# Picking the first rows by matrix multiply, and a first layer on the whole array, in the opening of a fused convolution and feed-forward kernel

## The chip, the cores and the metric

The kernel runs on one core of a Trainium2 chip. The metric is device time in microseconds (us) of one execution; the numbers are medians of several executions of the compiled program. The profile is of one execution by the hardware profiler. Its span starts and ends a little inside the timed interval (733.2 us of span for a run of 734.93).

PE is TensorE (matmuls), PEld its weight loads, ACT is ScalarE, DVE is VectorE, POOL is GpSimd, SP the sync engine, which here only issues DMAs.

## The reference, cut to what matters

```python
# x: (8, 4096, 192), weight_gen: (8, 4096, 8 heads, 7 taps), both float32
w = softmax(weight_gen, axis=-1)
x_pad = pad x by 6 zero rows in front of each sequence
out[b, s, h, :] = sum over k of w[b, s, h, k] * x_pad[b, s + k, h, :]     # 24 channels a head
h = relu(out.reshape(32768, 192) @ w_in)      # w_in  (192, 2048)
return (h * h) @ w_out                        # w_out (2048, 192)
```

Nearly all the arithmetic is in the two matrix products. The convolution has weights of its own for every position. The kernel turns it into matmuls as well, with a band of softmax weights as the moving operand.

## The kernel before: the parts that matter

The 32768 tokens are cut into sub-blocks of 512. The first two blocks are one sub-block each, so that work can start early; all later blocks are two. A block goes through these steps: softmax, rows of weights (`wr`), bands (`bd`), convolution (`yp` in PSUM, copied to `y`), 8 or 16 *units* of the first layer (`h`), each followed by a ScalarE relu (`t`) and a VectorE square (`g`), then the second layer (`o`).

The softmax has 8 consecutive positions in each partition. The bands need one position in each partition. In the kernel before, DMA does this re-arrangement (cuts are marked with `...`):

```python
def wr_load_sbuf(j, parts, order, engines):
    wr_t[j] = p_wr.tile([P, NT, HP, SL * 2], f16, name="wr")
    ...
    for i in order:                     # five overlapping tiles of 128 positions
        ...
        engines[n % len(engines)].dma_start(out=wr_t[j][a - t0 : b - t0, i]..., in_=s.v[...])
```

The opening, before the first block:

```python
spin(25)                                # warm-up matmuls on zeros
half_swap(); band_mask()
s0.load(nc.sync); load_w_in(w_st[0], 0, nc.sync); x_load_f32(0); load_w_in(w_st[1], 1, nc.sync)
s0.exp(...); s0.total(...); s0.recip(...); s0.scale(...)
nc.scalar.copy(out=w_i[:, 0, 0], in_=w_st[0])            # w_in, first half, float32 to float16
wr_load_sbuf(0, [s0], (0, 2, 1, 4, 3), (nc.sync, nc.gpsimd))
wr_load_sbuf(1, [s0], range(NT), (nc.gpsimd,))
x_cast(0, nc.scalar.copy)
cross_w_in_by_pe(0)                     # copy of w_in with its 64-row halves exchanged
spin(14)
x_load_f32(1)
nc.scalar.copy(out=w_i[:, 1, 0], in_=w_st[1])
cross_w_in(1)
...
```

A unit contracts over 192 rows in 64-row halves. Two 64-row matmuls lie side by side on the array, one working for each half of the tokens. This is why a crossed copy of w_in must exist:

```python
for jj in range(per):                   # per is 2 in the first two blocks
    for slot in range(NK):              # 3 slots of 64 rows
        for half, r0 in enumerate((0, RT)):
            k = slot ^ half if slot < 2 else slot
            nc.tensor.matmul(out=h[:, half, jj*th:(jj+1)*th], lhsT=w_in_chunk(...),
                             rhs=y_t[j][r0:r0+RT, k, 0:th], tile_position=(r0, 0), ...)
```

The softmax here doesn't subtract the row's maximum and nothing guards it: scores larger than these inputs give would overflow.

Of the kernel before, what the change touches and what calls it, by code (L numbers as in the profile page):

```python
# [9 lines left out]
def kernel(  # L10
# [26 lines left out]
    nc = tc.nc  # L37
    f32 = mybir.dt.float32
# [10 lines left out]
    PAIRED_FROM = 4  # L49
# [7 lines left out]
    NBLK = len(BLOCKS)  # L57
    NF = Dff // P
# [11 lines left out]
    bounds = [0, 104, 208, 312, 416, TB]  # L70

# [26 lines left out]
    swap = const.tile([P, P], f16, name="swap")  # L98
    FIRST = 8
    PARTS = {0: (8, 8, 8, 8), 1: (8, 8, 16), 2: (16, 16)}  # L100
# [5 lines left out]
    def half_swap():  # L106

        nc.gpsimd.memset(swap, 0.0)
        for base in (RT, -RT):
            nc.gpsimd.affine_select(  # L110
                out=swap, in_=swap, pattern=[[-1, P]], compare_op=AluOp.not_equal,
                fill=1.0, base=base, channel_multiplier=1,
            )
# [28 lines left out]

    def cross_w_in_by_pe(q):
        n = NQ + NQ // 2
        for a in range(0, n, 2 * TB):
            b = min(a + 2 * TB, n)
            pt = ps_h.tile([P, 2 * TB], f32, name="pt", tag="h")
            for c in range(a, b, TB):
                nc.tensor.matmul(
                    out=pt[:, c - a : c - a + TB], lhsT=swap, rhs=w_i[:, q, 0, c : c + TB],  # L150
                    start=True, stop=True,
                )
            nc.scalar.copy(out=w_i[:, q, 1, a:b], in_=pt[:, 0 : b - a])
# [147 lines left out]
    x_t, wr_t, bd_t, yp_t, y_t, g_t, gp_t, t1_t, o_t, o_sb_t = ({} for _ in range(10))  # L301
# [68 lines left out]

    def st_band(j, tiles):


        if j not in bd_t:
            bd_t[j] = p_bd.tile([P, H * NT * STEP], f16, name="bd")
        i = tiles[0]
        lo = STEP * i
        shift = 0 if i == 0 and j % NBB == 0 else lo - tile_start(j, i)
        n = min(STEP, P - shift)
        shape = (P, HP * len(tiles), n // SL, 2 * SL)  # L380
        nc.vector.tensor_tensor(  # L381
            out=bd_t[j][:, H * lo : H * (lo + len(tiles) * n)].rearrange(
                "p (g m c) -> p g m c", g=shape[1], c=2 * SL
            ),
            in0=wr_t[j][:, i : tiles[-1] + 1]
            .rearrange("p t g c -> p (t g) c")
            .unsqueeze(2)
            .broadcast_to(shape),
            in1=mask[:, shift : shift + n]
            .rearrange("p (m c) e -> p m (c e)", c=SL)  # L390
            .unsqueeze(1)
            .broadcast_to(shape),
            op=AluOp.mult,
        )
# [7 lines left out]
    def conv_pieces(j):  # L402


        s0, n = BLOCKS[j]
        th = n * TB // 2
        halves = []
        for half in (0, 1):
            s, a = (s0 + half, 0) if n == 2 else (s0, th * half)
            halves.append([  # L410
                (s, i, half, max(bounds[i], a), min(bounds[i + 1], a + th), a)
                for i in range(NT) if bounds[i] < a + th and bounds[i + 1] > a
            ])
        if n == 2:
            for k in range(NK):
                for later in (True, False):
                    for pair in zip(*halves):
                        for s, i, half, a, b, base in pair:
                            for q in (2 * k, 2 * k + 1):
                                yield later, s, i, q, half, a, b, base  # L420
        else:
            for pair in zip(*halves):
                for later in (True, False):
                    for k in range(NK):
                        for s, i, half, a, b, base in pair:
                            for q in (2 * k, 2 * k + 1):
                                yield later, s, i, q, half, a, b, base
# [38 lines left out]
    def st_conv(j):  # L466

        if j >= FIRST_SPREAD:
            return st_conv_spread(j)
        n = BLOCKS[j][1]  # L470
        th = n * TB // 2
        per = 1024 // th
        y = p_y.tile([P, NK, TB], f16, name="y")
        y_t[j] = y
        yps = [
            ps_h.tile([P, 2 * TB], f32, name="yp", tag="h") for _ in range(-(-NK // per))
        ]
        for later, s, i, q, half, a, b, base in conv_pieces(j):
            lo = bounds[i]
            hi = lo + (STEP if tile_start(s, i) == starts[i] else bounds[i + 1] - lo)  # L480
            _, ha, hb, pre = quads[q]
            m, h = (32, hb) if later else (pre, ha)
            bd = bd_t[s][:, H * lo : H * hi].rearrange("p (g c e) -> p g e c", g=HP, e=2)
            p0 = RT * half + 32 * (q % 2)
            k = q // 2
            col = th * (k % per) - base
            nc.tensor.matmul(  # L487
                out=yps[k // per][p0 : p0 + m, col + a : col + b],
                lhsT=x_t[s][:, i, 32 * q : 32 * q + m],
                rhs=bd[:, h // 2, h % 2, a - lo : b - lo],  # L490
                start=True,
                stop=True,
                skip_group_check=True,
                tile_position=(0, p0),
            )
        for n, yp in enumerate(yps):
            k0, k1 = n * per, min((n + 1) * per, NK)

            copies = ((k0, k1, nc.scalar.copy),)
            if j == 0:  # L500
                copies = ((0, 2, nc.scalar.copy), (2, NK, nc.vector.tensor_copy))
            for a, b, copy in copies:
                copy(  # L503
                    out=y[:, a:b, 0:th],
                    in_=yp[:, (a - k0) * th : (b - k0) * th].rearrange("p (k c) -> p k c", c=th),
                )

    def st_unit(j, u):

        th = BLOCKS[j][1] * TB // 2  # L510
        per = TB // th
        w = w_p if j >= FIRST_SPREAD else w_i
        h = ps_h.tile([P, 2, TB], f32, name="h", tag="h")
        for jj in range(per):
            for slot in range(NK):
                for half, r0 in enumerate((0, RT)):
                    k = slot ^ half if slot < 2 else slot
                    nc.tensor.matmul(  # L518
                        out=h[:, half, jj * th : (jj + 1) * th],
                        lhsT=w_in_chunk(w, u * per + jj, slot, half),  # L520
                        rhs=y_t[j][r0 : r0 + RT, k, 0:th],
                        start=(jj == 0 and slot == 0), stop=(slot == NK - 1),
# [10 lines left out]
        n = 2 if PAIRED_FROM <= j and u < NF - 2 else 1  # L533
# [14 lines left out]
    def st_mm2(j, qt, fcs, ccs, o):  # L548


        th = BLOCKS[j][1] * TB // 2
        per = TB // th
        half, off = divmod(qt * QT, th)
        for fc in fcs:
            g = g_t[(j, fc // per)][:, half, fc % per * th + off :]
# [39 lines left out]
    with nc.allow_low_precision("fp16 matmul pipeline"), tc.manual_schedule():  # L595
# [20 lines left out]
        nc.vector.memset(warm, 0.0)  # L616
        for v in v_first:
            nc.vector.memset(v, 0.0)
# [3 lines left out]
        def spin(n):  # L622
# [4 lines left out]
        spin(25)  # L627
        half_swap()
        band_mask()
        nc.gpsimd.memset(v_big, 0.0)  # L630
        s0.load(nc.sync)
        w_st = [
            p_wg.tile([P, (R + HALO) * HK], f32, name="w_st", tag="wg")[:, 0 : NQ + NQ // 2]
            for q in (0, 1)
        ]
        load_w_in(w_st[0], 0, nc.sync)
        x_load_f32(0)
        load_w_in(w_st[1], 1, nc.sync)
# [4 lines left out]
        nc.scalar.copy(out=w_i[:, 0, 0], in_=w_st[0])  # L643
        wr_load_sbuf(0, [s0], (0, 2, 1, 4, 3), (nc.sync, nc.gpsimd))
        wr_load_sbuf(1, [s0], range(NT), (nc.gpsimd,))
        x_cast(0, nc.scalar.copy)
        cross_w_in_by_pe(0)
        spin(14)
        x_load_f32(1)
        nc.scalar.copy(out=w_i[:, 1, 0], in_=w_st[1])  # L650
        cross_w_in(1)
        s1.load(nc.sync)
        for i in (0, 2, 1, 3, 4):
            st_band(0, (i,))
        st_conv(0)

        nc.gpsimd.tensor_copy(out=gate, in_=x_st[1][:, 0:1])
        for q in range(4):
            load_w_out(q, 4)
        s2.load(nc.gpsimd)  # L660
        x_load(2)

# [6 lines left out]
            0: "B1 X1 u u u E1 S1 u C u u u u",  # L669
            1: "L3 u u B2 M E2 B3 u M E2 u u S2 u M u C u S2 M",  # L670
            2: "L4 u u u E3 M u u u M B4 u u u u M B5 S3 u u u u M u E3 C u",
            3: "L5 L6 M S3 u u u M u u u u M u M B6 E4 u u u M M B7 u u u E4 M u M C S4 u",
# [95 lines left out]
        def quarters():  # L768

            for j in range(NBLK - 1):  # L770
                for qt in range(2 * BLOCKS[j][1]):
                    o = new_o(ps_o, 1, qt % 2) if j < 2 else new_o(ps_o)
                    st_mm2(j, qt, FCS[0], (0, 1), o)
                    yield
                    st_mm2(j, qt, FCS[1], (0, 1), o)
                    o_sum(j, qt, (0, 1), o)
                    if qt % 2:
                        o_store(j, qt - 1, range(4), nc.sync)
                    yield

        mm2 = quarters()
        for j in range(NBLK):
            if j + 2 < NBLK:
                load_rows(j + 2)
            u = 0
            for step in plans[j].split():
# [25 lines left out]
                elif kind == "X":  # L812
                    x_cast(n, nc.vector.tensor_copy)
# [47 lines left out]
```

## Time and profile before

| | kernel before |
|---|---|
| time, median | 734.86 us (734.37 to 736.79) |
| TensorE busy | 99% of the span |
| first unit of the first layer starts | 16.03 us |
| convolution of block 2 starts | 33.87 us |
| convolution of block 4 starts | 76.05 us |

The three last rows are marks. They are the starts of matmul groups in the timeline. Block 4 is the first that the two kernels reach with the same work behind them. What is left after that mark is the same in both.

The prediction shows the lines that say where the time lies. In the chain in order of time (start, us, what), three units in a row:

```profile
29.68 2.07 PE h L518 x36
```

That is 2.07 / 3 = 0.69 us a unit.

### The profile page before, as it was taken

Reading aid. Unit: us, or ns where it says so; the run is one execution under the profiler, and the core shown is the slowest. Engines: PE = TensorE matmul, PEld = TensorE weight load, DVE = VectorE, ACT = ScalarE, POOL = GpSimd, SP = SyncE. Lnnn points to the kernel's source line nnn. Section 1 sums busy time; section 2 is a strip of 40 time slices with the busy share of each in tenths; the row PEclk is TensorE's granted clock in tenths of the full one; section 3 lists DMA queues with packets and bytes.
Section 4 is the critical chain, followed back from the end, with each engine's and each line's share of the span. In section 5 each row is a group of like instructions: output and inputs, shape, how many; then the busy total and the mean of one; then the engine's idle time right before and its main releaser. Section 6 shows DMA issues by size and latency. Waiting matters only on the chain.

```text
span 733.2 us, 31124 instructions
## 1 busy us (share of the span) xinstructions
PE 726.3 (99%) x14106; PEld 528.5 (72%) x14106; DVE 627.3 (86%) x856; ACT 613.8 (84%) x724; POOL 100.5 (14%) x148
## 2 busy tenths in 40 slices
PE   8999999999999999999999999999999999999998
PEld 4767777777777777777777777777777777777777
DVE  5999898998898988888988888988889988778753
ACT  5998888988888888888888888888888888888883
POOL 7322222320001100011000010010100110001000
PEclk9999999999999999999999999999999999999999
DMA  7745444794445442455433464334544315444012
GB/s 216 124 88 132 81 63 106 143 164 119 93 73 117 105 86 64 71 131 112 69 70 72 115 125 82 62 68 122 104 87 85 59 49 120 66 87 78 30 45 67
DMA packets 126544, 68.71 MB, mean 94 GB/s; under 512 B 85193, under 2 KB 122636, under 8 KB 125900
## 3 DMA queue, kind: packets, MB, share of 16 engines
q1 hardware_dynamic: 80908, 48.12, 23.0%
q0 software_dynamic: 45360, 18.50, 21.6%
q8 instruction: 110, 1.80, 1.0%
q14 instruction: 22, 0.18, 0.1%
q10 hardware_dynamic: 144, 0.10, 0.0%
HBM read 50.18 MB, written 28.70 MB: 108 GB/s over the span
## 4 chain that ended last, share of the span: by engine, by line
PE 96%; DVE 1%; DMA 1%; ACT 1%; issue 0%; DVEq 0%
PE o L560 47%; PE h L518 45%; PE yp L450 4%; PE yp L487 1%; DVE bd L381 1%; DMA wr<-v_first 1%; ACT t L532 0%; DMA wg<-in_weight_gen_dram 0%; ACT ex L250 0%; DVE v_first L272 0%; ACT y L503 0%; DVE ssum L257 0%; DVE rcp L264 0%; DVE g L536 0%; DVE xt L347 0%
## 5 line engine op out<-in xcount | busy, mean ns | idle before, releaser
L532 ACT ACTIVATE t<-h 128x1024 f16<-128x1024 f32 x512 | 496.5, 1026 | 59.9 <-PE h L518 59.5
L560 PEld LDWEIGHTS <-g 64*128 64x128 f16 (+1 forms) x8032 | 342.5, 94 | 55.9 <-issue 2.5
L560 PE MATMUL o<-w_o,g 64*128 64x192 f16 (+1 forms) x8032 | 379.0, 243 | 0.0
L536 DVE TENSOR_TENSOR g<-t 128x2048 f16<-128x2048 f16 (+1 forms) x309 | 309.3, 1037 | 28.1 <-ACT t L532 27.9
L518 PE MATMUL h<-y,w_p 64*128 64x512 f16 x2400 | 291.7, 376 | 0.0
L518 PEld LDWEIGHTS <-w_p 64*128 64x128 f16 x2400 | 113.8, 94 | 94.9
L381 DVE TENSOR_TENSOR bd<-wr,mask 128x4160 f16<-128x4160 f16 (+3 forms) x89 | 149.4, 1703 | 4.1 <-DMA wr<-v_first 4.1
L576 DVE TENSOR_TENSOR o_sb<-o,o_sb 128x384 f32<-128x384 f32 x123 | 68.4, 556 | 60.8 <-ACT o_sb L574 59.8
L333 POOL DMA_DIRECT2D xt<-in_x_dram x62 | 52.1, 843 | 421.6 <-PE yp L450 362.5
L574 ACT COPY o_sb<-o 128x384 f32<-128x384 f32 x129 | 61.6, 478 | 46.7 <-PE o L560 45.9
L518 PE MATMUL h<-y,w_i 64*128 64x512 f16 (+1 forms) x768 | 82.1, 350 | 1.8 <-ACT t L532 0.8
L518 PEld LDWEIGHTS <-w_i 64*128 64x128 f16 x768 | 36.1, 94 | 28.6 <-issue 4.0
L450 PEld LDWEIGHTS <-xt 128*32 128x32 f16 x2000 | 24.5, 95 | 10.6 <-issue 10.6
L272 DVE TENSOR_TENSOR v_big<-ex,rcp 128x112 f16<-128x112 f32 (+5 forms) x180 | 29.8, 236 | 1.8 <-DMA vd<-v_big 0.8
L460 DVE CAST y<-yp 128x1024 f16<-128x1024 f32 x25 | 30.4, 1218 | 0.0
L450 PE MATMUL yp<-bd,xt 128*32 128x104 f16 (+1 forms) x2000 | 28.3, 210 | 0.0
L250 ACT ACTIVATE ex<-wg 128x560 f32<-128x560 f32 (+4 forms) x38 | 25.9, 682 | 1.7 <-DMA wg<-in_weight_gen_dram 1.7
L257 DVE TENSOR_REDUCE ssum<-ex 128x80 f32<-128x560 f32 (+4 forms) x38 | 25.3, 666 | 2.2 <-ACT ex L250 2.2
L460 ACT CAST y<-yp 128x1024 f16<-128x1024 f32 x25 | 25.2, 1006 | 0.0
L264 DVE RECIPROCAL rcp<-ssum 128x80 f32<-128x80 f32 (+4 forms) x38 | 22.8, 600 | 1.3
L323 POOL DMA_DIRECT2D xt<-in_x_dram x7 | 3.9, 553 | 124.7 <-PE yp L450 109.7
L363 POOL DMA_DIRECT2D wr<-v_first x31 | 16.9, 563 | 16.0 <-DVE v_first L272 15.8
(34 smaller groups left out, 97.3 us busy)
## 6 DMA issues: line engine op xcount, KB each, us to landing
out_dram<-o_sb SPq DMA_DIRECT2D x63, 384.0 KB
xt<-in_x_dram POOLq DMA_DIRECT2D x42, 240.0 KB, 5.0
wg<-in_weight_gen_dram SPq DMA_DIRECT2D x4, 1064.0 KB
xt<-in_x_dram POOLq DMA_DIRECT2D x20, 192.0 KB, 4.7
wr<-vd SPq DMA_DIRECT2D x38, 80.0 KB
vd<-v_big SPq DMA_DIRECT2D x5, 512.0 KB
y<-y SPq DMA_DIRECT2D x100, 24.0 KB
wg<-in_weight_gen_dram SPq DMA_DIRECT2D x5, 392.0 KB
```

The lines of the kernel that those rows point to most:

```text
L250: nc.scalar.activation(out=self.ex[:, lo:hi].rearrange("p r g k e -> p (r g) k e"), in_=self.wg[:, lo:hi].rearrange("p r (g e) k -> p (r g ...
L272: eng.tensor_tensor(out=bass.AP(tensor=v.tensor, offset=v.offset + lo * H * SL + lo % SL * 2 + g * SL * 2, ap=[list(v.ap[0]), [H * SL + 2, ...
L333: eng.dma_start(out=dst[:, first:last], in_=ap)
L381: nc.vector.tensor_tensor(out=bd_t[j][:, H * lo : H * (lo + len(tiles) * n)].rearrange("p (g m c) -> p g m c", g=shape[1], c=2 * SL), in0= ...
L450: nc.tensor.matmul(out=yp[p0 : p0 + 32, k - k0, a:b], lhsT=x_t[s][:, i, c0 : c0 + 32], rhs=bd[:, head // 2, e, 0 : b - a], start=True, sto ...
L460: copy(out=y[:, k0 : k0 + 2], in_=yp)
L518: nc.tensor.matmul(out=h[:, half, jj * th : (jj + 1) * th], lhsT=w_in_chunk(w, u * per + jj, slot, half), rhs=y_t[j][r0 : r0 + RT, k, 0:th ...
L532: nc.scalar.activation(out=t1[:, e], in_=h, func=ActF.Relu)
L536: nc.vector.tensor_tensor(out=g[:, a : e + 1], in0=t1[:, a : e + 1], in1=t1[:, a : e + 1], op=AluOp.mult)
L560: nc.tensor.matmul(out=oo[:, cc * Dm : (cc + 1) * Dm], lhsT=g[r0 : r0 + n, cc * P : (cc + 1) * P], rhs=w_o[r0 : r0 + n, fc, :], start=(fc ...
L574: nc.scalar.copy(out=o_sb, in_=o[0][:, c])
L576: nc.vector.tensor_tensor(out=o_sb, in0=o[1][:, c], in1=o_sb, op=AluOp.add)
```

## The change

Its intent is to bring the first useful matmul forward. The rows of the first two sub-blocks are picked by TensorE with a 0/1 selection matrix instead of by DMA. The first two blocks' units use the whole array for 128 of the 192 rows, so that no crossed copy of w_in is needed before block 2. The second half of w_in, x of the second sub-block and the second part of the softmax weights (a part serves two sub-blocks, so this one is for block 2) are loaded by GpSimd, the first two casting on the way. Squares are done two units at a time in all blocks. Some second-layer work moves from block 3 to block 0. The diff, cut to its core:

```diff
+    def select_rows(j, s, tiles, places):
+        ...
+        for i, (pool, tag) in zip(tiles, places):
+            pr = pool.tile([P, H * SL], f32, name="pr", tag=tag)
+            for r in range(s.r):                                  # 8
+                nc.tensor.matmul(out=pr, lhsT=sel[:, c : c + P], rhs=s.v[:, HALO + r]...,
+                                 start=(r == 0), stop=(r == s.r - 1))
+    def copy_rows(j, tiles):
+        for i in tiles:
+            nc.scalar.copy(out=wr_t[j][:, i]..., in_=pr_t.pop((j, i)))
...
+    def first_unit(u, h, y):
+        both  = [...]   # two 128-row matmuls of 512 columns
+        upper = [...]   # two 64-row matmuls of 512 columns, side by side
+        pairs = (upper, both) if u % 2 else (both, upper)
...
-        n = 2 if PAIRED_FROM <= j and u < NF - 2 else 1
+        n = 2 if j < NFIRST or u < NF - 2 else 1
...
-        spin(25)
-        half_swap()
+        spin(21)
+        row_select()
-        load_w_in(w_st[1], 1, nc.sync)
+        load_w_in(w_i[:, 1, 0], 1, nc.gpsimd)
+        x_load(1)
+        s1.load(nc.gpsimd)
-        wr_load_sbuf(0, [s0], (0, 2, 1, 4, 3), (nc.sync, nc.gpsimd))
-        wr_load_sbuf(1, [s0], range(NT), (nc.gpsimd,))
-        cross_w_in_by_pe(0)
-        spin(14)
+        select_rows(0, s0, ROW_ORDER, (o1, ring, ring, ring, o0))
+        copy_rows(0, ROW_ORDER)
+        def next_rows(i):                       # runs behind each tile of the convolution
+            select_rows(1, s0, (i,), ...)
+            if n < 2: copy_rows(1, (i,))
+            if n == 1: nc.scalar.copy(out=w_i[:, 0, 0], in_=w_st)
+        st_conv_first(0, next_rows)
...
-            0: "B1 X1 u u u E1 S1 u C u u u u",
+            0: "B1 u u u u E1 C S1 u u M u u",
```

## The prediction

> **What bounds the kernel now.** I read the page from the top: busy shares, slices, the chain that ended last, then that chain in order of time for the opening, then the timeline of the same stretch.
>
> From the page (engine, busy us, share, instructions; then the chain's shares):
>
> ```profile
> PE 726.3 (99%) x14106; PEld 528.5 (72%) x14106; DVE 627.3 (86%) x856; ACT 613.8 (84%) x724; POOL 100.5 (14%) x148
> ...
> PE   8999999999999999999999999999999999999998
> ...
> PE 96%; DVE 1%; DMA 1%; ACT 1%; issue 0%; DVEq 0%
> ```
>
> TensorE is busy in every slice, and 96% of the chain lies on it. So the end moves only if TensorE gets less to do, or starts useful work earlier, or waits less. But "busy" includes warm-up matmuls on zeros. The opening, in the chain in order of time (start, us, what), is not TensorE's at all:
>
> ```profile
> 0.82 3.00 DMA wg<-in_weight_gen_dram
> ...
> 3.84 0.94 ACT ex L250
> ...
> 4.80 0.98 DVE ssum L257
> ...
> 5.81 0.86 DVE rcp L264
> ...
> 6.70 1.47 DVE v_first L272 x8
> ...
> 8.19 3.98 DMA wr<-v_first
> ...
> 12.27 2.61 DVE bd L381 x5
> ...
> 14.92 0.45 PE yp L487 x16
> ...
> 15.40 0.59 ACT y L503
> ...
> 25.24 0.83 PE h L518 x12
> ```
>
> First a load, the softmax (done at 8.17), then 3.98 us of DMA that only re-arranges rows, 2.6 us for five bands, the tail of the convolution and its copy. The first useful first-layer matmul starts at 16.03. From 25.24 to the end the chain never leaves TensorE, and the waits view of TensorE from 25 to 730 us lists no wait at all. So the only time to win is before 25.24. What TensorE lost between 16.03 and 25.24: it did 108 first-layer matmuls (9 units of 12) and one 72-matmul convolution, 9 x 0.76 + 0.91 = 7.75 us of 9.21, so 1.46 us idle. The timeline of that stretch shows what held it:
>
> ```profile
> 16.36 2.35 DVE L381 TENSOR_TENSOR bd<-wr,mask 128x3328 f16<-128x3328 f16 x2
> ...
> 18.62 0.65 DVE L347 CAST xt<-x_st 128x960 f16<-128x960 f32 x1
> 19.19 1.89 DVE L536 TENSOR_TENSOR g<-t 128x1024 f16<-128x1024 f16 x3
> ...
> 22.28 5.66 ACT L532 ACTIVATE t<-h 128x1024 f16<-128x1024 f32 x6
> ```
>
> The second block's convolution waited for the DVE cast, and then eight units in a row ran at ScalarE's pace, about 0.95 us a unit, against TensorE's 0.76.
>
> **What the Trainium skill says.** (1) "TensorEngine Tiling (Array Packing)", Key Properties: changing the tiling mode drains TensorE. The trace agrees. Sixteen full-array second-layer matmuls take 1.43 us between 64-row units, and thirty-two 64-row ones 1.32 us; a run of three units is 2.05 us beside the full-array ones and 1.94 beside the 64-row ones. So a change of mode costs about 0.1 us. (2) "TensorE: Matmul & The Clock Gate", Back-to-back issue gap: a sustained stream of weight load plus matmul takes about 81 ns each at 128 columns. Here 16 such pairs at 192 columns take 1.43 us, 89 ns. The 64-column size that the change adds is not in this trace. (3) "DMA: Bandwidth & Descriptors", Anatomy of one DMA: a fixed cost of about 2 us, mostly completion. Here the 16 KB row moves land 3.0 us after issue and the chain pays 3.98, in agreement in kind. (4) The same page, SWDGE vs HWDGE vs iDMA: a casting DMA can only be issued from GpSimd. Before, casting loads of w_out from that queue took 6.2 us to land and those of x 4.8 to 6.1.
>
> **The change part by part.**
> *Rows by TensorE.* It takes 3.98 us of DMA off the chain. In its place, five tiles, each of eight matmuls (128x128 selection weights, 64 columns), and five ScalarE copies of 128x64. A copy, from 0.587 us at 512 and 1.005 at 1024 elements: 0.82 ns an element plus 0.17, so 0.22 us. A select matmul I take as an estimate of 55 ns: well under the 81 of the skill for 128 columns, since 64 columns stream in 27 ns and the weight load must set the pace. A 64-row load is shown to fit in 1.32/32 = 41 ns. That makes 0.44 us a tile, 2.2 us for one sub-block. Bands then follow copies, at 0.52 us each, hidden behind selects and convolution except the first.
> *Selects of the second sub-block* lie between the convolution's five tiles. Four of the five groups come before the last tile: 4 x 0.44 = 1.76 us on the path. They also change the mode between column tiles and full array eight times: 0.8 us. This is the price that I think the change pays for saving the second gather and its queue time.
> *Start.* The order of instructions has 21 warm-up matmuls first. Before, 14 ran at 427 ns to about 7.2 us and the rest at 213, so 21 end at 7.24 + 7 x 0.213 = 8.73, not 8.17: the selects start at about 8.75.
> *Sum to the first unit.* 8.75 + 2.2 (selects) + 0.1 + 5 x 0.18 (80 convolution matmuls in four column groups, 0.9) + 1.76 + 0.8 = 14.5, then 0.1 and a copy of 512 elements, 0.6 on ScalarE with the other half on DVE at the same time: 15.2. Before 16.03. Gain 0.8.
> *The w_in cast* (1.47 us, before on ScalarE at 8.06) now stands on ScalarE after seven row copies and before the y copy. Seven copies are done about 12.5, so it ends about 14.0: just hidden, if the staged w_in, now third in its queue, has landed by then. The second half of w_in comes by casting DMA: 1.47 us of ScalarE and the two TensorE swap steps (1.57 us of copies) go. They were hidden behind the row DMA, so nothing from the end.
> *Whole array.* A unit goes from 12 matmuls to 4 (two of 128 rows, two of 64 rows side by side, 512 columns): 3 x 0.213 = 0.64 us plus one change of mode of 0.1, against 0.69 to 0.76 before. So about nothing in TensorE time for 16 units, +-0.5. Its real worth is that no crossed copy of w_in is needed before block 2.
> *Paired squares.* 1.037 us for two units against 2 x 0.63: 0.2 us of DVE per pair, off the path after 25 us, some help before.
> *After the start.* ScalarE needs 8 x 0.98 for the units, 0.95 for the exp and 1.0 for y: 9.8 us, against TensorE 8 x 0.74 + 0.95 + 1.43 = 8.3, the second-layer half-quarter now standing in block 0. With three h buffers I walk the order through and lose 0.9 us before TensorE catches up, against 1.46: gain 0.5. No cast of x stands on DVE any more.
> *Behind the opening* each of the same matmuls remains, and TensorE is full there. Sum: 0.8 + 0.5 = 1.3 us. I add 1 us because my sizes for the select and for the mode changes may be high (a part of the drain hides behind waits for bands). 734.9 - 2.3 gives 732.6.
>
> **Rivals.** *A: selects are weight-load bound at 100 ns* (the profile's mean duration of a load is 94 to 98 ns, but it overlaps). 72 of them before the last convolution tile are then 3.2 us more: start 18.4, a time of about 736. For it: nothing in the trace has so short a matmul under full weights. Against: the 41 ns above. *B: a transfer takes the place of the wait.* GpSimd must first build a 1031-wide selection matrix and the mask (1.24 us for each 256-wide mask step, so 2 to 5 us for the new one), only then issues w_in's second half, x, and the second weights: landing at 15 to 19 us, where they are needed at about 18 to 20. If late by 2 us, ScalarE's exp holds units, and the time is about 735. For it: the queue's 4.8 to 8.1 us to landing. Against: there is slack of a microsecond or more for most. *C: the first unit at 13.5 and no stall at all*: selects at 45 ns with free mode changes. Then 2.5 + 1.5 = 4 us, 731. *D: the whole thing hidden* because TensorE's total is what counts: excluded by the 16 us before the first useful matmul.
>
> **Range and chances.** Even the best case, start at 13 and no loss, wins 4.5 us, 0.6%; rival A with late transfers loses 4 us. A 2% step is 14.7 us, nearly all that lies before the first unit, so within 2% is almost sure: 0.98, and 0.01 each for the others. Time 732.6, eight in ten within 730.2 to 735.2: low end rival C and a little more, high end rival B.
>
> **What would show it.** The selects' groups should take 0.44 us per eight, the first select start near 8.75, the first unit near 15.2, in the chain no DMA between the softmax and the bands. TensorE's waits after the first unit should sum to about 1 us and end by block 1; units of blocks 0 and 1 should keep 0.7 to 0.76 us; from block 2 on every stage should be as long as before. I am wrong if the chain shows a wait for w_in, x, weights or the mask, if a select costs 100 ns, or if a gap appears after 40 us, such as the bands of block 2 coming late because their row moves start later.

## The result, and the profile after

The changed kernel takes 733.07 us (732.70 to 733.32, 6 runs), beside 735.16 for the kernel before in the same rounds. The ratio is 0.9969, with a 95% interval of 0.9956 to 0.9982: 0.3% less, so "same" at the 2% threshold. A ratio is the mean time of one kernel's fast runs over that of the other's of the same rounds, so it is not quite the ratio of the medians.

| mark (us from the span's start) | before | changed | difference |
|---|---|---|---|
| softmax of the first part done | 8.17 | 8.46 | +0.29 |
| first unit starts | 16.03 | 13.72 | -2.31 |
| convolution of block 4 starts | 76.05 | 74.30 | -1.75 |
| span | 733.2 | 731.5 | -1.7 |

The start gains 2.31 us, 0.56 is given back by block 4, and nothing moves after that. The opening, from the timeline of the changed kernel (start us, us, engine line op, out<-in, count, and in brackets the idle time before and what ended it):

```profile
8.51 1.27 PE L368 MATMUL pr<-v_first,sel 128*128 128x64 f16 x38 [0.41 <-DVE v_first L260]
9.05 0.97 ACT L377 CAST wr<-pr 128x64 f16<-128x64 f32 x5
9.37 2.60 DVE L391 TENSOR_TENSOR bd<-wr,mask 128x832 f16<-128x832 f16 x5 [0.91 <-ACT wr L377]
...
10.11 0.37 PE L447 MATMUL yp<-bd,xt 128*32 128x104 f16 x16 [0.33 <-ACT wr L377]
10.41 0.41 PE L368 MATMUL pr<-v_first,sel 128*128 128x64 f16 x8
10.74 0.37 PE L447 MATMUL yp<-bd,xt 128*32 128x104 f16 x16
...
11.60 1.48 ACT L708 CAST w_i<-w_st 128x1536 f16<-128x1536 f32 x1
...
13.08 0.59 ACT L459 CAST y<-yp 128x512 f16<-128x512 f32 x1
...
13.70 0.69 DVE L460 CAST y<-yp 128x512 f16<-128x512 f32 x1 [1.73 <-ACT y L459]
13.72 3.38 PE L549 MATMUL h<-y,w_i 128*128 128x512 f16 x16 [0.35 <-ACT y L459]
...
17.03 1.12 PE L447 MATMUL yp<-bd,xt 128*32 128x104 f16 x80
...
18.08 1.68 PE L549 MATMUL h<-y,w_i 128*128 128x512 f16 x8
```

Thirty-eight selects take 1.27 us. The first band starts 0.91 us after the softmax ended, where it was 12.27 - 8.17 = 4.1 us before. The five bands take the same 2.60 us as before. Convolution tiles follow one another every 0.64 us, with a group of selects between them. At 13.08 the w_in cast ends, and the y copy starts in the same moment.

The waits view of TensorE from 13.8 to 62 us (engine line waited for: us in total, times, longest) lists every wait with a name from the first unit on:

```profile
PE h L549 <- ACT y L459: 0.3, 1, 0.3
PE yp L519 <- DVE bd L391: 0.3, 1, 0.3
PE o L613 <- DVE o_sb L629: 0.2, 1, 0.2
PE h L564 <- ACT y L530: 0.2, 1, 0.2
```

The first of them is the wait for the first unit itself. The second is at 32.5 us, for the bands of block 2. Followed back from 60 us, the chain view goes to what these bands waited for, their rows by DMA (25.63 to 28.99 us). The control below, the same program, does not have this wait; it has the other two.

But the units have become longer. Three in a row in the timeline, and the second-layer group behind them:

```profile
27.54 2.43 PE L549 MATMUL h<-y,w_i 64*128 64x512 f16 x12
...
29.81 1.48 PE L613 MATMUL o<-w_o,g 128*128 128x192 f16 x16
```

From start to start that is 29.81 - 27.54 = 2.27 us, or 0.757 us a unit against 0.69 before. (The 2.43 holds the drain of the last matmul, which overlaps the next group.)

### The profile page after: what moved, and what is told of

It is laid out like the page before. It is cut to its first block, busy times and chain, and to the rows that moved or that the text cites. A ratio compares the mean times of both kernels' runs of the same rounds, so it can differ in the third digit from the quotient of the medians.

```text
span 731.5 us, 30985 instructions
## 1 busy us (share of the span) xinstructions
PE 724.6 (99%) x14053; PEld 529.2 (72%) x14053; DVE 626.1 (86%) x834; ACT 612.8 (84%) x731; POOL 100.0 (14%) x145
## 4 chain that ended last, share of the span: by engine, by line
PE 92%; DVE 2%; issue 1%; DMA 0%; ACT 0%; DVEq 0%
PE o L613 45%; PE h L564 42%; PE yp L485 4%; PE yp L519 1%; DVE bd L391 1%; DVE g L582 1%; DMA wr<-v_first 0%; ACT t L578 0%; DVE v_first L260 0%; DVE rcp L252 0%; DVE ssum L245 0%; PE h L549 0%; DVE o_sb L629 0%; ACT o_sb L627 0%; DVEq L391 0%
## 5 line engine op out<-in xcount | busy, mean ns | idle before, releaser
L564 PE MATMUL h<-y,w_i 64*128 64x512 f16 x576 | 70.8, 376 | 0.2 <-ACT y L530 0.2
L564 PEld LDWEIGHTS <-w_i 64*128 64x128 f16 x576 | 31.2, 94 | 21.4 <-issue 1.4
L351 POOL DMA_DIRECT2D wr<-v_first x24 | 12.9, 562 | 22.8 <-ACT t L578 12.2
```

The costliest lines, as they stand in the source:

```text
L564: nc.tensor.matmul(out=h[:, half], lhsT=w_in_chunk(w, u, slot, half), rhs=y_t[j][r0 : r0 + RT, k], start=(slot == 0), stop=(slot == NK - 1 ...
```

## The experiments

Twelve kernels ran, all timed in five rounds against the kernel before. The first row repeats the result above, from rounds of its own. The diffs are cut to the lines that matter. "First unit" and "block 4" are the marks defined above. The time from the first unit to block 4's convolution was 60.02 us before and 60.58 in the changed kernel.

| run | time, us | ratio to before, 95% interval | first unit | block 4 |
|---|---|---|---|---|
| changed kernel | 733.07 | 0.9969 (0.9956 to 0.9982) | 13.72 | 74.30 |
| rows by DMA again | 739.22 | 1.0058 (1.0044 to 1.0072) | 19.38 | 80.70 |
| three full matmuls a unit (wrong result) | 731.88 | 0.9961 (0.9948 to 0.9973) | 13.33 | 72.50 |
| six 64-row matmuls a unit (wrong result) | 732.69 | 0.9970 (0.9957 to 0.9982) | 13.33 | 73.24 |
| single squares | 733.38 | 0.9980 (0.9967 to 0.9992) | 13.65 | 73.87 |
| plain loads | 734.99 | 0.9993 (0.9981 to 1.0006) | 13.83 | 75.92 |
| old plan | 733.07 | 0.9974 (0.9961 to 0.9986) | 13.43 | 73.88 |
| y tiles apart | 732.90 | 0.9967 (0.9955 to 0.9980) | 13.28 | 73.62 |
| selects late | 732.95 | 0.9966 (0.9952 to 0.9979) | 13.32 | 73.48 |
| changed kernel again (control) | 732.95 | 0.9976 (0.9958 to 0.9993) | 13.54 | 73.90 |
| rows by sync engine | 739.10 | 1.0055 (1.0039 to 1.0070) | 17.81 | 79.42 |
| selects alone, on the kernel before | 736.62 | 1.0018 (1.0002 to 1.0034) | 15.65 | 76.72 |
| start improved | 732.19 | 0.9964 (0.9948 to 0.9979) | 12.92 | 73.23 |

The first four experiments shared their runs of the kernel before, so did the next four, and so did the last four. The middle four ran on another chip than the other eight, so the ratio, and not the time alone, compares them. Two limits should be kept in mind. The first load lands up to 0.4 us earlier or later from run to run, and the first unit moves with it: 13.72 and 13.54 are the same program. And from block 4 to the end the profiles differ by up to 1.4 us (657.2 us before and in the changed kernel, 658.5 with the old plan), though the work there is the same. I found no cause for this. So differences under about 0.7 us in time decide nothing alone, and the marks are read with them.

My theory, A: the start comes from the selects, and a change of tiling mode within each unit gives part of it back. Rivals: the start comes from the loads having moved, or ScalarE's pace (about 0.95 us a unit) sets the opening whatever TensorE does.

### Rows by DMA again, in two forms

```diff
-        select_rows(0, s0, ROW_ORDER, (o1, ring, ring, ring, o0))
-        copy_rows(0, ROW_ORDER)
+        wr_load_sbuf(0, [s0], (0, 2, 1, 4, 3), (nc.sync, nc.gpsimd))
+        wr_load_sbuf(1, [s0], range(NT), (nc.gpsimd,))
-        spin(21)
+        spin(37)
```

In the second form all ten moves are issued by the sync engine, in the order of the tiles.

> The changed kernel with the rows of both first sub-blocks moved by DMA again, all else kept. Theory A (the selects on TensorE are what brings the first unit from 16.03 to 13.72 us): the first unit starts 2 to 3.5 us later, at about 16 to 17 us, and the kernel takes 735 to 736.5 us, 2 to 3.5 more than changed. Rival (the start comes from the other loads having moved to other queues): the first unit stays below 15 us and the time within 1 us of changed.

> A fairer form of rows by DMA in the changed kernel: all ten row moves from the sync engine, so that none stands behind the casting loads, as the slow ones did in the first attempt (first unit 19.38 us). Theory A (selects are faster in themselves, and row moves also suffer from the casting loads that now fill the transfer engines at that time): first unit at 15.5 to 17.5 us and 735 to 737 us. Rival (the first attempt lost by its queue alone): first unit at 14 to 15 us and within 1 us of the control.

Measured: 739.22 and 739.10 us. Both are 6 us above the changed kernel and more than 4 above the kernel before in the same rounds; the direction is theory A's and the size beyond what I expected of either. In the first form half the moves stand on GpSimd's queue behind the casting loads, so that trial said too little. The second form has no such excuse. The bands' wait for rows and TensorE's wait for bands, from its timeline:

```profile
12.25 0.59 DVE L391 TENSOR_TENSOR bd<-wr,mask 128x832 f16<-128x832 f16 x1 [4.03 <-DMA wr<-v_first]
...
14.38 2.18 DVE L391 TENSOR_TENSOR bd<-wr,mask 128x832 f16<-128x832 f16 x4 [1.54 <-DMA wr<-v_first]
...
17.81 5.23 PE L549 MATMUL h<-y,w_i 128*128 128x512 f16 x16 [0.68 <-ACT y L459]
```

The first band comes as late as in the kernel before (12.25 against 12.27 us); the other four, which followed at once there, wait another 1.54 us here. The first unit is 4.3 us later than in the control (13.54). The four units that follow then take 22.97 - 17.81 = 5.16 us, where the changed kernel needs 17.03 - 13.72 = 3.31. The windows view names the reason. (Columns: stretch, its length, then busy us and count of PE, PEld, DVE, ACT and POOL, the granted clock, DMA share and GB/s.)

```profile
8.00:11.40 3.40, 3.37 (x16) 1.43 (x15) 0.22 (x2) 1.47 (x1) 3.40 (x7) 1.00 1.11 154
11.40:17.80 6.40, 2.30 (x80) 1.57 (x80) 2.79 (x6) 0.59 (x1) 2.28 (x5) 0.82 1.57 231
17.80:23.00 5.20, 5.19 (x20) 0.94 (x23) 3.85 (x4) 2.86 (x3) 3.19 (x2) 0.57 0.71 126
```

TensorE was mostly idle for 6.4 us, and its granted clock was 0.57 while the first units ran. A late start was paid twice: 4.3 us of waiting and 1.85 us of slow units. Of this 0.6 comes back by block 4, which is reached 5.52 us later than in the control. The medians differ by 6.15; the other 0.6 appears behind that mark, where I found no cause. The Trainium skill has the clock's part ("TensorE: Matmul & The Clock Gate", Part 1: an idle window of about 3.4 us brings the array back to half its clock), and the trace agrees: in finer windows, TensorE was busy for 0.37 us from 11.4 to 15.0, and from 15.5 to 22.0 the granted clock was 0.50. So beside saving time the selects keep the array from idling. The slow units belong to this experiment and not to rows by DMA as such: its 37 warm-up matmuls ended at 11.4 us, where the kernel before kept TensorE on warm-up work to 13.3. The rival that moving the loads brought the start is refuted: with the loads moved and the rows by DMA the start is worse than before.

### Three full-array matmuls a unit, and six 64-row ones

Their outputs are wrong, which doesn't matter for the times. The first replaces the pair of 64-row matmuls by one of 128 rows:

```diff
-            (h[:, n], w_i[r0 : r0 + RT, q, 0, NQ + f * P :][:, 0:P], y[r0 : r0 + RT, 1], r0)
-            for n, r0 in enumerate((0, RT))
+            (h[:, n], w_i[:, q, 0, NQ + f * P :][:, 0:P], y[:, 1], 0)
+            for n in (1,)
```

The second replaces the two 128-row matmuls by two pairs of 64-row ones, each row half writing to its own half of `h`.

> Wrong result on purpose: a unit of blocks 0 and 1 is three full-array matmuls of 512 columns, with no pair of 64-row matmuls, so no change of tiling mode in a unit, and the same array time of 0.64 us. Theory A (a change of mode inside each of 16 units costs about 0.1 us, and this ate the 1.5 us of waits that the change removed): a unit takes 0.65 us instead of 0.76 to 0.83, and the kernel 731.3 to 732.3 us, 0.8 to 1.8 less than changed. Rival B (ScalarE's 0.95 us for each unit sets the pace of the opening): units shorten on TensorE, but it waits as much more, and the time stays within 0.4 us of changed.

> Wrong result on purpose: a unit of blocks 0 and 1 is six 64-row matmuls of 512 columns in three pairs, the form that later blocks have, at the same array time; modes change only at the full-array second layer. Theory A: a unit takes 0.65 to 0.70 us and the kernel 0.5 to 1.5 us less than changed, a little less gain than with three full ones, as each second-layer group then starts with a change of mode. Rival B: within 0.4 us of changed.

Measured: 731.88 and 732.69 us. The time that the array streams is the same 0.64 us a unit in all three forms. With three full matmuls, three units in a row:

```profile
26.70 2.11 PE L549 MATMUL h<-y,w_i 128*128 128x512 f16 x9
28.64 1.48 PE L613 MATMUL o<-w_o,g 128*128 128x192 f16 x16
```

28.64 - 26.70 = 1.94 us, or 0.647 a unit against 0.757: 0.11 us less for one change of mode less. From the first unit to block 4 it took 72.50 - 13.33 = 59.17 us, 1.41 less than changed and 1.19 less than the control (60.36). The medians say 1.1 to 1.2. Sixteen units at 0.11 would be 1.76; part of it is not realised. The rival "ScalarE's pace alone" had said 0.4 us at most, and falls.

It is not wholly wrong, though. In this run the first four units, up to the second convolution, still took 16.45 - 13.33 = 3.12 us, 0.78 each. Their third matmul starts at about 14.1, just after VectorE's half of y is there (14.00), and the rest run without a gap. The convolution starts at 16.45, just after the second relu ends (about 16.4) and frees a PSUM buffer. In the changed kernel the same stretch is 3.31 us, so removing the mode change brings only 0.19 there. It costs in full where TensorE is the bound and is partly hidden where y or ScalarE is.

With six 64-row matmuls, units took 0.68 us and the stretch to block 4 59.91 us. That is 0.45 less than the control, a miss in time: 732.69 us is within the noise of the control, and the ratio doesn't separate them. Taken alone, this run is 0.38 us below the changed kernel and so lies in the rival's range; it is the form with three full matmuls that decides.

A correct form of the six would cross the row halves: rows 0 to 63 first add to one half of `h` and then to the other. Two row tiles of the array would write the same PSUM bank with nothing ordering them. "TensorEngine Tiling (Array Packing)", Restrictions and Gotchas, states this rule; no run here shows the failure itself. That is why the change takes the 128-row form and bears its mode change.

### Single squares

```diff
-        n = 2 if j < NFIRST or u < NF - 2 else 1
+        n = 2 if j >= 4 and u < NF - 2 else 1
```

> Only the paired squares of blocks 0 to 3 are undone. Each single square is about 0.63 us against 1.04 to 1.1 for a pair, so 0.15 to 0.2 us of VectorE per pair. Theory A (VectorE is off the path but for the bands of block 2): the bands of block 2 come up to 0.8 us later, time 0 to 0.6 us more than changed. Rival: earlier single squares release the second layer sooner, and the time is the same or up to 0.5 us less.

Measured: 733.38 us, ratio 0.9980, and 60.22 us from first unit to block 4. It is not told apart from the changed kernel (0.9969 and 0.9976 in its two runs). One wait grows: a second-layer group in block 3 waits 0.62 us instead of 0.20 for VectorE's sum. The later bands of block 2 that theory A expected do not show: no wait for them is left, but the control has none either. Pairing the squares in the first blocks has no effect that these runs can measure.

### Plain loads

```diff
-        load_w_in(w_i[:, 1, 0], 1, nc.gpsimd)
-        x_load(1)
-        s1.load(nc.gpsimd)
+        load_w_in(w_st1, 1, nc.sync)            # float32, cast on ScalarE after two units
+        x_load_f32(1); s1.load(nc.sync)         # x cast on VectorE
```

> Second half of w_in, x of sub-block 1 and its softmax weights by plain loads from the sync engine again, with the casts on ScalarE (1.47 us) and VectorE (0.65 us). Theory A (these loads are hidden before, but a cast on ScalarE now stands among the first relus, which are back to back there from 14.9 us): first unit as in the changed kernel, at 13.5 to 14 us, time 0.8 to 1.6 us more. Rival: the loads are hidden either way and TensorE's three h buffers absorb the cast, within 0.4 us of changed. Second rival: the casting queue was late, so plain loads make it faster.

Measured: 734.99 us, ratio 0.9993: 1.7 us of the gain is gone. The start is the same, as theory A had it. The loss is behind it, from the timeline:

```profile
16.81 1.47 ACT L880 CAST w_i<-w_st 128x1536 f16<-128x1536 f32 x1
17.43 0.92 DVE L335 CAST xt<-x_st 128x960 f16<-128x960 f32 x1 [0.66 <-DMA x_st<-in_x_dram]
...
18.41 1.11 PE L447 MATMUL yp<-bd,xt 128*32 128x104 f16 x80 [1.20 <-DVE xt L335]
```

The second convolution waits 1.20 us for the cast of x, which itself waits for its load (0.66 us idle before it), so this load was not hidden, as theory A had assumed. ScalarE has 1.47 us of cast among the relus. This experiment moves three loads and two casts together and doesn't part them. (The expectation gives the softmax weights to sub-block 1; they are those of block 2.)

### The old plan

```diff
-            0: "B1 u u u u E1 C S1 u u M u u",
+            0: "B1 u u u u E1 C S1 u u u u",
-            3: "L5 L6 S3 u u u M ...
+            3: "L5 L6 M S3 u u u M ...
```

> The quarter of second-layer work that stands in block 0 goes back to block 3. Theory A (in block 0 ScalarE has more to do than TensorE, so this work fills idle time): TensorE then waits about 1 to 1.4 us in blocks 0 and 1, time 0.7 to 1.4 us more than changed. Rival: mode changes have made TensorE's units nearly as long as ScalarE's, so that there was no idle time to fill: within 0.4 us.

Measured: 733.07 us, ratio 0.9974; the rival's answer. TensorE does wait in block 0 without the second-layer work:

```profile
20.12 3.69 PE L549 MATMUL h<-y,w_i 128*128 128x512 f16 x16 [0.66 <-ACT y L462]
```

But the two waits of the changed kernel at 54 and 60 us are then gone (0.17 and 0.20 us), and the time from the first unit to block 4 is 60.45 us, against 60.58 and 60.36. The 0.66 us is made up elsewhere.

### The halves of y in tiles of their own

```diff
-        y = p_y.tile([P, NK, TB], f16, name="y")
+        y = [p_one.tile([P, TB], f16, name=f"ya{n}") for n in (0, 1)]    # block 0
```

> The two halves of block 0's y in tiles of their own, so that VectorE's copy needn't follow ScalarE's (it waited 1.73 us and started at 13.70, as ScalarE's ended). If the order comes from the shared tile, VectorE's copy starts at about 13.1 us and ends before ScalarE's, the 64-row matmuls of the first unit start 0.1 to 0.3 us sooner, and the bands of block 1 some 0.6 us sooner; time 0.1 to 0.5 us less. If the two copies are ordered by the shared PSUM tile, nothing changes.

Measured: 732.90 us, and VectorE's copy still started (13.27) as ScalarE's ended (12.65 + 0.59 = 13.24). The second case held: the order is not from the `y` tile. The last experiment leaves the shared PSUM tile as what made it.

### Selects late

```diff
-        st_conv_first(0, next_rows)
-        copy_rows(1, ROW_ORDER[2:])
+        st_conv_first(0)
+        ...                                     # 40 selects into one PSUM bank
+        nc.scalar.copy(out=wr_t[1]..., in_=pr)  # one copy of 320 elements
```

The cast of w_in's first half goes to just behind the first sub-block's row copies.

> The selects of sub-block 1 go behind block 0's convolution, into the time in which y is copied, with one ScalarE copy of 320 elements (estimate 0.43 us) for five, and the cast of the first half of w_in comes before that. Theory A (selects and the w_in cast, which ended at 13.08 as the y copy began, stand on the path to the first unit): the convolution follows the bands (last one at 12.0 us), y is copied from 12.5, first unit at 13.1 us instead of 13.7, time 0.4 to 0.8 us less than changed. Rival: bands of block 1 come later by as much, or the w_in load isn't there yet at 10 us, and it is within 0.3 us.

Measured: 732.95 us. The y copy now starts at 12.26, but the first unit only at 13.32, as the 40 selects (12.14 to about 13.4) stand before it on TensorE. The first unit comes 4.87 us after the softmax's end (8.45), against 5.26 changed and 5.11 in the control: 0.24 to 0.39 us, about half of the 0.6 that I expected. The time doesn't show it.

### Selects alone, on the kernel before

```diff
-        wr_load_sbuf(0, [s0], (0, 2, 1, 4, 3), (nc.sync, nc.gpsimd))
+        select_rows(0, s0)                      # 40 selects, one ScalarE copy
```

> The kernel before, with the rows of the first sub-block alone picked on TensorE (one ScalarE copy of 320 elements), and no other part of the change. Theory A (the parts need one another: with the crossed w_in and both casts of w_in still on ScalarE, that engine becomes the next wait): copy done at about 10.0 us, bands at 12.6, but ScalarE works through x, the crossed copies and the second w_in cast until about 14, so the first unit comes at 14.6 to 15.2 us instead of 16.03, and the time is 0.6 to 1.6 us less than before. Rival (the selects alone bring it all): first unit by 13.9 us and 2 us less than before.

Measured: 736.62 us, ratio 1.0018: no gain at all, where theory A had 0.6 to 1.6 us. The start did move, by 0.4 us to 15.65 (0.54 counted from the softmax's end, 8.33 here). ScalarE in the timeline:

```profile
10.45 0.43 ACT L136 CAST wr<-pr 128x320 f16<-128x320 f32 x1 [1.37 <-PE pr L131]
10.77 0.99 ACT L370 CAST xt<-x_st 128x960 f16<-128x960 f32 x1
11.66 1.50 ACT L176 CAST w_i<-pt 128x1024 f16<-128x1024 f32 x2
13.04 1.49 ACT L675 CAST w_i<-w_st 128x1536 f16<-128x1536 f32 x1
15.02 0.59 ACT L526 CAST y<-yp 128x512 f16<-128x512 f32 x1 [0.48 <-PE yp L510]
```

Once the DMA is gone, ScalarE is busy with casts and crossed copies from 10.45 to 14.53. TensorE meanwhile runs its 14 warm-up matmuls (to about 14.0), which I had left in; they, not ScalarE, set the convolution's start at 14.01. So the claim that the parts need one another holds in this measure: the selects alone bring 0.4 of the 2.3 us. That ScalarE would have come next is argued and not shown: as an estimate, with the warm-up gone it is free for the y copy at 14.53, and the first unit could start at about 15.1. From the first unit to block 4 it took 61.07 us, 1.05 more than before. Of this 0.61 is TensorE's idle time (1.99 us against 1.38 in the windows view): the second convolution waits 0.47 us for the cast of x instead of 0.26, the units 0.88 for a relu instead of 0.78, and the bands of block 2 cost 0.21. The other 0.44, and 1.0 us behind block 4, stay open.

### The start improved

```diff
+        if j == 0:
+            yps[1] = ps_o.tile([P, TB], f32, name="yp1", tag="o0")     # a PSUM tile of its own
+        nc.scalar.copy(out=w_i[:, 0, 0], in_=w_st)                     # ahead of the y copy
+            for i in {0: (0,), 2: (1,), 4: (2, 3, 4)}.get(n, ()):      # selects: 2 tiles within, 3 behind
```

> The changed kernel with the first w_in cast ahead of the y copy, the selects of sub-block 1 two tiles within the convolution and three behind it, one copy of 320 elements for them, and the two halves of y in PSUM tiles of their own (separate y tiles alone left the order as it was). If the shared PSUM tile ordered the copies, VectorE's now runs beside ScalarE's. First unit 0.4 to 0.7 us sooner after the softmax's end than in the control (about 12.9 to 13.2 us). As ScalarE has no gap from its first relu to about 26 us, the time should follow the first relu: 0.3 to 0.8 us less than the control. Rival: later bands or the transfers of block 2 take it back, within 0.2 us.

Measured: 732.19 us, ratio 0.9964, beside 732.95 and 0.9976 for the control of the same rounds.

```profile
12.28 0.59 ACT L462 CAST y<-yp 128x512 f16<-128x512 f32 x1 [0.82 <-PE yp L450]
12.34 0.69 DVE L463 CAST y<-yp 128x512 f16<-128x512 f32 x1 [0.48 <-PE yp L450]
12.92 3.18 PE L552 MATMUL h<-y,w_i 128*128 128x512 f16 x16
```

The two copies now run side by side: with the y tile excluded by the experiment above, the shared PSUM tile had ordered them. (This run changes two more things, the places of the cast and of the selects.) The first unit starts 4.57 us after the softmax's end (8.35) instead of 5.11, and block 4's convolution 0.67 us sooner than in the control. The medians differ by 0.76 us, as expected; the intervals overlap, so the traces carry this more than the times. It gives a correct result and has the lowest median of the correct kernels.

## Why the prediction was right, point by point

The time, 733.07, lies in the range and 0.5 us from the point. The mechanism was right; three sizes were off, and they partly cancel, so that the total came this close is in part luck. By its own terms:

- **Start.** Predicted 15.2 us, measured 13.72: a gain of 2.31 instead of 0.8. *The select* was sized at 55 ns and is 1.27 / 38 = 33 ns: 1.3 us for a sub-block, not 2.2. *Selects between convolution tiles*: predicted 1.76 us and 0.8 for eight mode changes. Measured, a tile and its selects take 0.64 us. The second block's convolution has 80 matmuls in 18.08 - 17.03 = 1.05 us, 0.21 a tile. Eight selects at 32 ns are 0.26. That leaves about 0.18 for two mode changes, 0.09 each. So the mode changes were sized right, and the excess was the select: 40 before the convolution and 32 in it, at 22 ns too much, is 1.6 us, about the 1.5 us between 15.2 and 13.72. The other terms nearly cancel: the selects began 0.24 sooner, the first tile came 0.23 later than the sum had it, and the last tile took 0.18 more. The extra 1 us that I took off "because my sizes for the select and for the mode changes may be high" was right for the select, but its size was a guess. The sentence that the weight load must set the pace was wrong, and the 89 ns that I read beside it held a change of mode: sixteen such pairs without one take 31.13 - 29.81 = 1.32 us in the changed kernel, 82 ns, where 192 columns stream in 80.
- **Start of the selects.** Predicted 8.75, set by the warm-up; measured 8.51, set by the softmax. The warm-up ended at 7.38, as more of its matmuls ran at full clock. Near the right number for the wrong reason.
- **The w_in cast "just hidden".** It ended at 13.08, not 14.0, and is the very instruction that the y copy followed. Hidden, but with nothing to spare: the last convolution tile had ended at 13.03.
- **Whole array.** This is the step that failed: "0.64 us plus one change of mode of 0.1, against 0.69 to 0.76 before. So about nothing". The 0.74 was right (0.757). The comparison was not: undisturbed units before took 0.69, and the 0.76 I set beside it were units next to a full-array group. Sixteen units at 0.067 us are 1.07 us more work on TensorE. The windows view agrees: from the first unit to block 4 TensorE was busy for 58.64 us before and 59.69 in the changed kernel and its control, but 58.27 with three full matmuls. Removing the mode change gave back 1.1 to 1.4 us on the chip. Nor did the units "keep 0.7 to 0.76 us": the first four took 0.83 each, and one alone before a second-layer group 26.11 - 25.26 = 0.85.
- **After the start.** Predicted 0.9 us of waiting against 1.46, gain 0.5. TensorE's idle time is 20.64 - 20.11 = 0.53 us from the first unit to the end of block 2's convolution (windows view), and 0.37 in blocks 2 and 3: 0.9. Before, the same view gives 1.38 from 16.03 to 35.44. Right in size, but not in the place: the last waits came at 54 and 60 us, in blocks 2 and 3, not by block 1. A gap after 40 us was one of the prediction's signs of being wrong; it came, at 0.17 and 0.20 us.
- **Paired squares.** The 1.037 us was a mean of pairs and singles. By shape, a pair takes 1.220 and a single 0.688 us, so 0.16 is saved and not 0.2; no run tells the difference in time.
- **Sum.** 2.31 + 0.48 - 1.07 = 1.72 us, against 1.75 at block 4 in the traces and 2.1 between the medians. The prediction's 0.8 + 0.5 + 1.0 = 2.3 came near because the start was too small and the whole array's cost was left out.
- **Rivals.** A (selects at 100 ns) is refuted by 33 ns. B (a transfer takes over) did not occur for the loads that it named; the nearest to it is the 0.30 us for block 2's bands, whose rows come by DMA; they kept TensorE waiting in one of two profiles of the program. C (start 13.5, no stall) came near the start, but by other sizes: it had selects at 45 ns, not 33, and took mode changes as free. The selection matrix that I put at 2 to 5 us on GpSimd took 1.05.

## What to carry to other kernels

A small re-arrangement (here five moves of some 16 KB) that stands on the critical path can be cheaper as narrow matmuls with a 0/1 matrix than as a DMA: here 1.3 us and a copy for 4 us. But take out what stands next in line in the same step (here 14 warm-up matmuls), or the gain stops there. When a change swaps the shape of matmuls, compare its units with undisturbed units of the kernel before and count the mode changes: 0.067 us a unit, sixteen times, was nearly half as much as the start had won. And a longer wait at the start is paid again if the array's clock falls during it.

## What the Trainium skill lacked or had wrong

- "TensorE: Matmul & The Clock Gate", Back-to-back issue gap: it gives about 81 ns for a stream of weight load and matmul at 128 columns, and nothing for a stream of narrower ones with fresh weights (its row for 1 to 64 columns is of the matmul alone). Here 38 matmuls of 64 columns, each with new 128x128 weights, took 1.27 us, 33 ns each. Scaling from the 81 misled the prediction (it took 55).
- "TensorEngine Tiling (Array Packing)", Key Properties: it says that a change of mode drains the array, without a size. Here it cost 0.11 us in a unit (0.757 against 0.647) and about 0.09 between column tiles and the full array.
- No page that I read gives the time of GpSimd's affine select. Here 1031 float16 columns in one run took 1.05 us, and 256 in a two-level pattern 1.24 (mean of the two mask steps before).
- No page that I read says that two engines' reads of different banks of one PSUM tile come out ordered in a kernel written like this. VectorE's copy waited 1.73 us for ScalarE's, and ran beside it with a tile of its own. So here the order came from the program and was not a limit of the chip.
